# The head of the last product: GpSimd makes the sums of four weight chunks, and c's last pair but one takes its sums in another order

## The chip, the cores and the metric

One core of a Trainium2 chip runs the whole program. The metric is the device time of one execution in microseconds, the median of several. TensorE (PE) multiplies, VectorE (DVE), ScalarE (ACT) and GpSimd (POOL) do the elementwise work, and SyncE (SP) issues the transfers. Every engine works through its own list of instructions in order; an instruction whose operand isn't ready holds up everything behind it on its engine.

## The reference

```python
attn = softmax(causal(q @ k.T / 8)) @ v        # 2 x 12 heads, 448 x 64
x = attn, as 896 tokens x 768
h = x @ w_in;  g = h * cos(h)                  # 768 -> 2048
y = g @ w_out                                  # 2048 -> 768
a = y @ w_a;   b = y @ w_b                     # 768 -> 1536 each
out = (a * b) @ w_o2                           # c = a * b;  1536 -> 768
```

All of it is in float32. The last product (o2 in the kernel) is `c @ w_o2`.

## The kernel before

**Two halves.** A float32 operand is used as a pair: hi, the value rounded to the matmul's type, written by ScalarE, and lo, the rest, written by VectorE or GpSimd. One block product is three matmuls: hi by hi, hi by lo, lo by hi. So nothing is multiplied before the hi and lo of both sides are there.

**Weights.** They arrive as 88 chunks, numbered i in the order of use; the last product has 18 of them, from `o2_first` = 70 on, six for each of its three column pairs p. A chunk lies in HBM as 64-bit numbers. For each one: `w_scale` (two ScalarE instructions, the second into a PSUM tile named top, of which there is one), `w_bits` (two VectorE instructions, line 202), `w_sums` (below), `w_hi` (ScalarE, in two parts of 384 and 512 columns) and `w_lo` (GpSimd, the same two parts). When `w_lo(i)` is done, the load of chunk i+4 is issued into the same place. The calls are written out by hand among the matmuls: `halves_of(i)` makes `w_bits` up to i, the scale of the next one and then hi and lo of i; `bits_to(i)` makes only the scales and bits up to i.

**Seven products for eight.** The last product and most of `a` multiply 2x2 blocks with seven products. It needs sums of blocks on both sides. For a chunk, `w_sums` (lines 144 to 150) makes them in three instructions, each of which needs the one before: a difference of 128x128, two sums at once in 128x256, and a difference of 128x128. In the kernel before VectorE makes all three for a chunk of the last product. For c, each pair q = 0..5 of row blocks has four blocks (b11, b12, b21, b22) and the sums t1, t3, t2, t4.

**c.** a is made first and kept; each product b_q lands in four PSUM banks and is multiplied with a. For q from 3 on (`c_mult_psum`) b12 is multiplied in its PSUM bank, and `sum_psum` makes t3 in b12's bank, and t2 and then t4 in b22's bank. `half` makes hi and lo: from PSUM with VectorE, from SBUF with GpSimd. `steps_of` is the list of these steps ("+t2" the sum, "t2" its hi and lo), taken from `todo` by `items(n)`. t4 overwrites t2 in its bank, so it must wait until t2's halves are made.

**PSUM.** `bank(next(cycle), ...)` hands out seven banks in turn. The last product opens seven products at once. By that cycle its b11, t2 and t3 get the banks of b12, b21 and b22 of q = 4; its t1 and b21 those of b11 and b21 of q = 5; and its b22 and t4 those of b12 (which holds t3) and b22 (which holds t2, then t4) of q = 5. A product can't begin before VectorE has read its bank for the last time.

**The place.** Of the products a and b, b_4 and b_5 are the last. b_5 is multiplied in two batches, first b11 and b21, then b12 and b22 (lines 861 to 882). At the head of the last product (lines 898 to 911) c's last pair q = 5 is split, and TensorE multiplies all seven products for chunks 70 and 71 (42 matmuls), then chunks 72 and 73 (21 each), then 74 and 75 in turn. Places for new tiles of c come from the list `free`, first in, first out.

Of the kernel before, what the change touches and what calls it, by code (L numbers as in the profile page):

```python
# [14 lines left out]
ALU = mybir.AluOpType  # L15
# [15 lines left out]
def tile_causal_attention_cos_gate_bilinear(  # L31
# [16 lines left out]
    nc = tc.nc  # L48
# [5 lines left out]
    N_IN, N_Y, N_Q = w_in.shape[0], w_out.shape[0], w_a.shape[0]  # L54
# [17 lines left out]
    T_Y = N_Y // 2  # L72
    FIRST_PLAIN = 1
    AB = [("a", 0), ("b", 0), ("a", 1), ("b", 1), ("a", 2), ("a", 3), ("b", 2), ("a", 4), ("a", 5), ("b", 3), ("b", 4), ("b", 5)]
# [66 lines left out]
    def w_sums(i):  # L141


        if is_seven(*queue[i][:2]):
            t = f32(raw[i]).rearrange("p (s n) w -> p s w n", s=4)
            nc.vector.tensor_tensor(out=t[:, 0, 1], in0=t[:, 0, 0], in1=t[:, 1, 0], op=ALU.subtract)  # L146
            a22 = t[:, 2, 0].unsqueeze(1).to_broadcast([P, 2, P])
            nc.vector.tensor_tensor(out=t[:, 1:3, 1], in0=t[:, 0], in1=a22, op=ALU.add)  # L148
            engine = nc.gpsimd if i < o2_first else nc.vector
            engine.tensor_tensor(out=t[:, 3, 1], in0=t[:, 3, 0], in1=t[:, 2, 1], op=ALU.subtract)  # L150

    def w_parts(i):

# [51 lines left out]
    def w_halves(i):  # L205

        w_hi(i)
        w_lo(i, nc.gpsimd)
# [131 lines left out]
    with ExitStack() as actx:  # L340
# [11 lines left out]
        for o in (0, S):  # L352
            for e in range(2):
                half = mask[e * D : (e + 1) * D, o : o + D]
                nc.gpsimd.affine_select(
                    out=half,
# [232 lines left out]
    with tc.manual_schedule():  # L589
# [35 lines left out]
        def get(kind, q, name, part=""):  # L625
            return tiles[kind, q, name, part][0]
# [24 lines left out]
        def items(n):  # L651
            while n and todo:
                if next(todo[0], todo) is todo:
                    todo.popleft()
                else:
                    n -= 1
# [50 lines left out]
        def bits_to(i):  # L707
            while bits[0] <= i:
                scale_next()
                w_bits(bits[0])  # L710
                bits[0] += 1

        def halves_of(i):
            bits_to(i)
            scale_next()
            w_halves(i)
# [41 lines left out]
        def multiply_plain(kind, p, q, batches, use):  # L758
            for r in range(2):
                for b in batches:  # L760
                    name = name_of(r, b)
                    if q == 0:
                        banks[name] = bank(next(cycle), f"{kind}_{name}")[:, :S]
                    for k in range(2):
                        x_pair = pair_of("y", q, name_of(k, b))
                        terms(banks[name], chunks[kind, p, q][:2], BLOCK[r, k], x_pair, q == k == 0, q == T_Y - 1 and k == 1)
                    if q == T_Y - 1:
                        use(p, name, banks[name])
# [6 lines left out]
            nc.vector.tensor_tensor(out=t, in0=ps, in1=t, op=ALU.mult)  # L775

        in_psum = {}

        def c_mult_psum(p, name, ps):

            if name[2] == "2":
                in_psum[p, name] = ps
            if name == "b12":
                nc.vector.tensor_tensor(out=ps, in0=ps, in1=get("c", p, name), op=ALU.mult)
                drop("c", p, name)
            else:
                c_mult(p, name, ps)

        def sum_psum(q, name):
            t3, t2 = in_psum[q, "b12"], in_psum[q, "b22"]  # L790
            if name == "t1":
                ops = make("c", q, "t1"), t3, get("c", q, "b11")
            elif name == "t3":
                ops = t3, t3, get("c", q, "b22")
            elif name == "t2":
                ops = t2, get("c", q, "b11"), t3
            else:
                ops = t2, get("c", q, "b21"), t2
            nc.vector.tensor_tensor(out=ops[0], in0=ops[1], in1=ops[2], op=ALU.subtract)  # L799

        def half(q, name, dve):
            key = {"t3": "b12", "t2": "b22", "t4": "b22"}.get(name)
            src = in_psum[q, key] if (q, key) in in_psum else get("c", q, name)
            engine = nc.vector if name in dve or (q, key) in in_psum else nc.gpsimd
            split(src, (make("c", q, name, "hi"), make("c", q, name, "lo")), engine)
            if (q, key) not in in_psum:
                drop("c", q, name)

        def steps_of(q, steps, dve=()):
            for step in steps.split():  # L810
                if step[0] == "+":
                    sum_psum(q, step[1:])
                else:
                    half(q, step, dve)
                yield
# [9 lines left out]
        for turn, (kind, p) in enumerate(AB[:-1]):  # L825
            banks, kept = {}, {}
            for q in range(T_Y):
                halves_of(n + 3)
                bits_to(n + 4)
                items(PER_QUAD[turn])  # L830
                if n == o2_first - T_Y - 1:
                    bits_to(n + 5)
                if is_seven(kind, p):
                    for name in OPS:
                        multiply(kind, p, q, [name], "y", T_Y)
                        if q == T_Y - 1:
                            take(name, banks[name], lambda m: make("c", p, m), lambda m, t: None)
                else:
                    use = a_copy if kind == "a" else c_mult if p < OWN else c_mult_psum
                    multiply_plain(kind, p, q, ALL, use)  # L840
                del chunks[kind, p, q]
                n += 1
            if kind == "b" and p < OWN:
                split_c(p, () if p < 2 else ("b11", "b21", "b22"))
            elif kind == "b":
                todo.append(steps_of(p, "+t1 +t3 +t2 t2 +t4 t3 t4 b11 b21 b22 t1"))
                items(3)
            if (kind, p) == ("a", N_Q - 1):
                for t in range(T_Y):
                    for name in T_NAMES:  # L850
                        for part in ("hi", "lo"):
                            drop("y", t, name, part)
        assert n + T_Y == o2_first

        def drop_batch(b):
            for t in range(T_Y):
                for m in range(2):
                    for part in ("hi", "lo"):
                        drop("y", t, name_of(m, b), part)
# [1 line left out]
        banks = {}  # L861
        last = N_Q - 1
        for q in range(T_Y):
            items((2, 1, 0)[q])
            if q == 0:
                halves_of(o2_first)
            if q == 1:
                bits_to(o2_first + 2)
            multiply_plain("b", last, q, [0], c_mult_psum)
        drop_batch(0)  # L870
        for q in range(T_Y):
            if q == 1:
                scale_next()
            items((3, 2, 0)[q])
            if q == 1:
                bits_to(o2_first + 3)
            multiply_plain("b", last, q, [1], c_mult_psum)
            del chunks["b", last, q]
            if q < 2:
                w_halves(o2_first + 1 + q)  # L880
# [17 lines left out]
        for p in range(T_Y):  # L898
            banks, kept = {}, {}
            i = o2_first + p * N_Q  # L900
            if p == 0:
                todo.append(steps_of(last, "+t1 +t3 +t2 t2 +t4 t3 t4 b11 b21 b22 t1", ("b21",)))
                w_halves(i + 3)
                items(7)
                bits_to(i + 4)
                items(4)
                all_done()
                for name in OPS:
                    for q in range(2):
                        multiply("o2", p, q, [name], "c", N_Q)  # L910
                del chunks["o2", p, 0], chunks["o2", p, 1]
                halves_of(i + 4)
            for q in range(0 if p else 2, DOUBLE):
                halves_of(i + q + 3)
                if (p, q) not in ((0, 3), (1, 0), (1, 1)):
                    bits_to(i + q + 4)
                multiply("o2", p, q, OPS, "c", N_Q)
                del chunks["o2", p, q]
            for step, name in enumerate(OPS):
                for q in range(DOUBLE, N_Q):  # L920
                    multiply("o2", p, q, [name], "c", N_Q)
                take(name, banks[name], result, lambda m, t: store(p, m, t))
                if step == (5 if p == 0 else 0):
                    halves_of(i + DOUBLE + 3)
                if step == 6 and p:
                    bits_to(i + N_Q + 2)
            for q in range(DOUBLE, N_Q):
                del chunks["o2", p, q]
            halves_of(i + N_Q + 2)
            if p:  # L930
                bits_to(i + N_Q + 3)
# [56 lines left out]
```

## Time and profile before

| | us |
|---|---|
| median of 3 runs | 568.85 |
| lowest and highest | 567.16, 568.89 |
| the profiled execution | 566.28 |
| its span in the trace | 564.5 |
| TensorE busy | 552.3 |
| VectorE busy | 413.4 |
| ScalarE busy | 327.2 |
| GpSimd busy | 314.5 |

The span runs from the first to the last instruction of the trace, and the profiled execution's own time is 1.8 us longer. All times of instructions below are from the span's start. Busy time is summed over the whole span; where a wait lies is told by the view of waits and by the lists in order of time.

### The profile page before, as it was taken

What the parts mean: (1) busy time and instruction counts of PE and PEld (TensorE: products, weight loads), DVE (VectorE), ACT (ScalarE), POOL (GpSimd) and SP (SyncE); (2) the same over time, 40 slices, a digit from 0 to 9 for tenths busy, and PEclk for the clock granted to TensorE, in tenths of its full rate; (3) what the DMA queues carried; (4) which work ended last, traced back from release to release, by engine and by line L of the source; (5) the groups of instructions that cost most, each with busy time, mean ns of one, the idle gap of its engine ahead of it and who ended that gap; (6) DMA issues with size and microseconds to landing.
All of it is one profiled execution on the core that took longest, in us unless ns stands there. A gap on an engine that the chain in (4) does not pass through costs nothing.

```text
span 564.5 us, 9012 instructions
## 1 busy us (share of the span) xinstructions
PE 552.3 (98%) x3195; PEld 493.1 (87%) x3195; DVE 413.4 (73%) x752; ACT 327.2 (58%) x675; POOL 314.5 (56%) x307
## 2 busy tenths in 40 slices
PE   8999999999999999999999999999999999599997
PEld 5676689999999999999999999999999999599996
DVE  5899937777777775753742768898787878879994
ACT  6888937777777743322233865675544546545650
POOL 4557743666666652322231895998552656655651
PEclk9999999999999999999999999999999999799999
DMA  8845211333333234342441335244344321334431
GB/s 320 303 135 220 91 57 57 111 113 111 112 107 99 89 119 149 95 130 76 131 148 39 112 84 177 77 133 128 111 121 140 108 82 47 102 113 144 145 103 66
DMA packets 18045, 67.82 MB, mean 120 GB/s; under 512 B 2000, under 2 KB 3664, under 8 KB 18000
## 3 DMA queue, kind: packets, MB, share of 16 engines
q1 hardware_dynamic: 18000, 67.25, 36.6%
q8 instruction: 25, 0.41, 0.3%
q14 instruction: 20, 0.16, 0.1%
HBM read 64.49 MB, written 2.75 MB: 119 GB/s over the span
## 4 chain that ended last, share of the span: by engine, by line
PE 84%; DVE 7%; ACT 4%; issue 2%; POOL 2%; POOLq 0%; DVEq 0%; ACTq 0%
PE h L232 21%; PE y L232 21%; PE b_b L746 9%; PE a_b L746 7%; PE o_t L746 7%; PE a_t L746 6%; PE o_b L746 6%; PE xa L507 2%; PE pt L480 2%; PE s L405 2%; POOL p L467 1%; DVE p L428 1%; ACT p L452 1%; DVE b_b L799 1%; DVE c_b L775 1%
## 5 line engine op out<-in xcount | busy, mean ns | idle before, releaser
L175 POOL TENSOR_TENSOR w_lo<-w_raw,w_hi 128x512 fp32r<-128x512 f32 (+2 forms) x121 | 168.6, 1402 | 164.2 <-ACT w_hi L168 124.4
L168 ACT ACTIVATE w_hi<-w_raw 128x384 fp32r<-128x384 f32 (+2 forms) x118 | 80.0, 688 | 137.9 <-DVE w_raw L137 38.2
L114 ACT ACTIVATE w_raw<-w_raw 128x512 f32<-128x512 f32 (+1 forms) x88 | 65.2, 741 | 0.6 <-DMA w_raw<-in_w_b 0.6
L130 DVE SCALAR_TENSOR_TENSOR w_raw<-w_raw 128x768 int32<-128x768 int32 (+1 forms) x34 | 52.9, 1556 | 16.4 <-ACT w_raw L114 15.5
L467 POOL TENSOR_SCALAR p<-p,sums 128x448 f32<-128x448 f32 (+6 forms) x84 | 40.7, 505 | 26.9 <-DVE mn L428 25.5
L202 DVE SCALAR_TENSOR_TENSOR top<-w_raw,top 128x512 int32<-128x512 int32 x54 | 37.2, 688 | 18.8 <-ACT top L119 18.1
L119 ACT ACTIVATE top<-w_raw 128x512 int32<-128x512 uint32 x54 | 34.0, 630 | 26.1 <-DVE w_raw L202 25.5
L452 ACT ACTIVATE p<-p,mn 128x448 f32<-128x448 f32 (+6 forms) x84 | 41.8, 501 | 7.8 <-DVE mn L428 7.8
L202 DVE SCALAR_TENSOR_TENSOR w_raw<-w_raw,top 128x512 int32<-128x512 int32 x54 | 37.2, 690 | 5.4
L272 DVE SCALAR_TENSOR_TENSOR r<-r,h 128x448 f32<-128x448 int32 x32 | 19.7, 616 | 25.8 <-ACT r L271 25.7
L428 DVE CUSTOM_DVE_ANT_0 p<-s,mask 128x448 f32<-128x448 f32 (+6 forms) x84 | 32.0, 415 | 3.8 <-PE s L405 3.6
L137 DVE SCALAR_TENSOR_TENSOR w_raw<-w_raw 128x768 int32<-128x768 int32 (+1 forms) x34 | 31.6, 931 | 0.4
L405 PE MATMUL s<-qk_raw 64*64 64x448 f32 (+6 forms) x336 | 26.8, 390 | 0.7 <-DVE mn L428 0.5
L148 DVE TENSOR_TENSOR w_raw<-w_raw 128x256 f32<-128x256 f32 x33 | 25.5, 774 | 1.1
L271 ACT ACTIVATE r<-h 128x448 int32<-128x448 f32 x32 | 17.2, 540 | 15.9 <-PE h L232 8.2
L405 PEld LDWEIGHTS s<-qk_raw 64*64 64x64 f32 x336 | 15.2, 132 | 11.2 <-issue 3.7
L480 PE MATMUL pt<-ident,p 128*128 128x128 f32 x168 | 23.9, 280 | 1.0 <-POOL p L467 0.6
L507 PEld LDWEIGHTS xa<-pp,v 128*64 128x64 f32 x336 | 16.1, 137 | 9.4 <-issue 7.1
L507 PE MATMUL xa<-pp,v 128*64 128x64 f32 (+3 forms) x336 | 23.8, 293 | 0.0
L146 DVE TENSOR_TENSOR w_raw<-w_raw 128x128 f32<-128x128 f32 x33 | 22.5, 681 | 1.1
L480 PEld LDWEIGHTS pt<-ident,p 128*128 128x128 f32 x168 | 18.2, 140 | 3.7 <-POOL p L467 2.0
L124 DVE TENSOR_SCALAR w_raw<-w_raw 128x768 int32<-128x768 int32 (+1 forms) x34 | 21.2, 623 | 0.0
(374 smaller groups left out, 1717.3 us busy)
## 6 DMA issues: line engine op xcount, KB each, us to landing
w_raw<-in_w_in SPq DMA_DIRECT2D x16, 768.0 KB, 4.4
w_raw<-in_w_out SPq DMA_DIRECT2D x12, 768.0 KB, 4.3
w_raw<-in_w_a SPq DMA_DIRECT2D x18, 512.0 KB, 3.6
w_raw<-in_w_b SPq DMA_DIRECT2D x18, 512.0 KB, 3.6
w_raw<-in_w_o SPq DMA_DIRECT2D x18, 512.0 KB, 3.8
v<-in_v SPq DMA_DIRECT2D x12, 448.0 KB, 5.8
qk_raw<-in_qk SPq DMA_DIRECT2D x11, 448.0 KB, 5.7
w_raw<-in_w_out SPq DMA_DIRECT2D x6, 512.0 KB, 3.8
```

The source lines that it names most:

```text
L114: nc.scalar.activation(high, high, ACTF.Copy, scale=2.0**-112)
L130: nc.vector.scalar_tensor_tensor(out=low, in0=high, scalar=3, in1=low, op0=ALU.logical_shift_left, op1=ALU.bitwise_or)
L168: nc.scalar.activation(pair[0][:, a:z], src, ACTF.Copy)
L175: engine.tensor_tensor(out=lo[:, a:z], in0=src, in1=f32(hi)[:, a:z], op=ALU.subtract)
L202: nc.vector.scalar_tensor_tensor(out=out_, in0=high, scalar=by, in1=top, op0=op, op1=ALU.bitwise_or)
L232: nc.tensor.matmul(ps, w[:, c * P : (c + 1) * P], acts[t + c][part], start=t == 0 and i == 0, stop=t + k == n and i == len(terms) - 1,)
L405: nc.tensor.matmul(T["s", i + c][q, o : o + WIDTH[j]], t[h, Q_COL[j] : Q_COL[j] + D], t[h, FIRST[j] : FIRST[j] + WIDTH[j]], start=True, st ...
L452: nc.scalar.activation(t, t, ACTF.Exp, bias=T["mn", n][:, c], scale=-1.0, accum_out=row_sum(n, j))
L467: nc.gpsimd.tensor_scalar(out=t, in0=t, scalar1=row_sum(n, j), scalar2=1.0, op0=ALU.mult, op1=ALU.mult)
L480: nc.tensor.transpose(dst, p_bufs[n % N_P][:, o : o + P], ident)
L507: nc.tensor.matmul(ps[e * D : (e + 1) * D, o * D : w * D], t[:, k, e], p[:, :, :, q].rearrange("p s l q -> p (s l) q") if k < 3 else p[:, ...
L746: nc.tensor.matmul(ps, w_part, x_part, start=start and i == 0, stop=stop and i == 2)
```

## The change

`w_sums`: for the first four chunks of the last product (70 to 73) GpSimd makes all three sums; from chunk 74 on VectorE does, as before. For the chunks of `a` VectorE makes the first two and GpSimd the third, as before.

c's pair q = 4: t4 goes into b21's PSUM bank and no longer overwrites t2, so all four sums are made at once; the order of the steps behind them is another. In the products b_3 and b_4 the steps of c are issued ahead of `bits_to`. `items` and `bits_to` of b_5's two batches are moved, `free` is turned so that the places that the first batch gives up are used first, and at the head of the last product the seven first steps of q = 5 come ahead of `w_halves` of chunk 73.

```diff
             a22 = t[:, 2, 0].unsqueeze(1).to_broadcast([P, 2, P])
-            nc.vector.tensor_tensor(out=t[:, 0, 1], in0=t[:, 0, 0], in1=t[:, 1, 0], op=ALU.subtract)
-            nc.vector.tensor_tensor(out=t[:, 1:3, 1], in0=t[:, 0], in1=a22, op=ALU.add)
-            engine = nc.gpsimd if i < o2_first else nc.vector
-            engine.tensor_tensor(out=t[:, 3, 1], in0=t[:, 3, 0], in1=t[:, 2, 1], op=ALU.subtract)
+            most = nc.gpsimd if o2_first <= i < o2_first + 4 else nc.vector
+            last = nc.vector if i >= o2_first + 4 else nc.gpsimd
+            most.tensor_tensor(out=t[:, 0, 1], in0=t[:, 0, 0], in1=t[:, 1, 0], op=ALU.subtract)
+            most.tensor_tensor(out=t[:, 1:3, 1], in0=t[:, 0], in1=a22, op=ALU.add)
+            last.tensor_tensor(out=t[:, 3, 1], in0=t[:, 3, 0], in1=t[:, 2, 1], op=ALU.subtract)
...
+        T4_BANK = {q: "b21" if q == N_Q - 2 else "b22" for q in range(N_Q)}
...
-                ops = t2, get("c", q, "b21"), t2
+                ops = in_psum[q, T4_BANK[q]], get("c", q, "b21"), t2
...
                 halves_of(n + 3)
+                if turn == len(AB) - 2:
+                    items(PER_QUAD[turn])
                 bits_to(n + 4)
-                items(PER_QUAD[turn])
-                if n == o2_first - T_Y - 1:
+                if turn < len(AB) - 2:
+                    items(PER_QUAD[turn])
+                elif q == T_Y - 1:
                     bits_to(n + 5)
...
-                todo.append(steps_of(p, "+t1 +t3 +t2 t2 +t4 t3 t4 b11 b21 b22 t1"))
-                items(3)
+                order = "+t1 +t3 +t2 t2 +t4 t3 t4 b11 b21 b22 t1"
+                todo.append(steps_of(p, order if p < N_Q - 2 else "+t1 +t3 +t2 +t4 b11 b21 t3 t2 t4 b22 t1"))
+                items(3 if p < N_Q - 2 else 4)
...
         for q in range(T_Y):
-            items((2, 1, 0)[q])
             if q == 0:
                 halves_of(o2_first)
+                items(2)
             if q == 1:
                 bits_to(o2_first + 2)
             multiply_plain("b", last, q, [0], c_mult_psum)
+        k = len(free)
         drop_batch(0)
+        free.rotate(-k)
         for q in range(T_Y):
-            if q == 1:
+            if q == 0:
                 scale_next()
             items((3, 2, 0)[q])
-            if q == 1:
+            if q == 2:
                 bits_to(o2_first + 3)
...
+                items(7)
                 w_halves(i + 3)
-                items(7)
```

**VectorE, between c's pair q = 4 and the last sums of q = 5.** c_b, c_t are tiles of c, b_b the PSUM banks of b, L146 to L150 the sums of a chunk, L202 its bits. Before:

```order
L212 TENSOR_TENSOR c_t4lo<-b_b_4545,c_t4hi 128x448
L202 SCALAR_TENSOR_TENSOR top<-w_raw,top 128x512
L202 SCALAR_TENSOR_TENSOR w_raw<-w_raw,top 128x512
L146 TENSOR_TENSOR w_raw<-w_raw 128x128
L148 TENSOR_TENSOR w_raw<-w_raw 128x256
L150 TENSOR_TENSOR w_raw<-w_raw 128x128
L784 TENSOR_TENSOR b_b_4731<-b_b_4731,c_b_4327 128x448
L775 TENSOR_TENSOR c_b_4338<-b_b_4738,c_b_4338 128x448
L799 TENSOR_TENSOR c_t_4808<-b_b_4731,c_b_4322 128x448
L799 TENSOR_TENSOR b_b_4731<-b_b_4731,c_b_4338 128x448
L799 TENSOR_TENSOR b_b_4738<-c_b_4322,b_b_4731 128x448
L212 TENSOR_TENSOR c_t2lo<-b_b_4738,c_t2hi 128x448
```

The same place now, on the same engine:

```order
L213 TENSOR_TENSOR c_t4lo<-b_b_4538,c_t4hi 128x448
L203 SCALAR_TENSOR_TENSOR top<-w_raw,top 128x512
L203 SCALAR_TENSOR_TENSOR w_raw<-w_raw,top 128x512
L785 TENSOR_TENSOR b_b_4734<-b_b_4734,c_b_4327 128x448
L776 TENSOR_TENSOR c_b_4338<-b_b_4741,c_b_4338 128x448
L800 TENSOR_TENSOR c_t_4801<-b_b_4734,c_b_4322 128x448
L800 TENSOR_TENSOR b_b_4734<-b_b_4734,c_b_4338 128x448
L800 TENSOR_TENSOR b_b_4741<-c_b_4322,b_b_4734 128x448
L213 TENSOR_TENSOR c_t2lo<-b_b_4741,c_t2hi 128x448
```

The three sums of chunk 73 are gone from between its bits and the products of c's pair q = 5; what follows stands in the same order.

**GpSimd, from the lo of chunk 69 to the lo of chunk 71.** w_lo is a chunk's lo, c_b11lo and c_b21lo those of c's pair q = 4. Before:

```order
L175 TENSOR_TENSOR w_lo<-w_raw,w_hi 128x512
L175 TENSOR_TENSOR w_lo<-w_raw,w_hi 128x384
L175 TENSOR_TENSOR w_lo<-w_raw,w_hi 128x512
L212 TENSOR_TENSOR c_b11lo<-c_b_4210,c_b11hi 128x448
L212 TENSOR_TENSOR c_b21lo<-c_b_4220,c_b21hi 128x448
L175 TENSOR_TENSOR w_lo<-w_raw,w_hi 128x384
```

And now:

```order
L151 TENSOR_TENSOR w_raw<-w_raw 128x128
L176 TENSOR_TENSOR w_lo<-w_raw,w_hi 128x384
L176 TENSOR_TENSOR w_lo<-w_raw,w_hi 128x512
L213 TENSOR_TENSOR c_b11lo<-c_b_4210,c_b11hi 128x448
L213 TENSOR_TENSOR c_b21lo<-c_b_4220,c_b21hi 128x448
L149 TENSOR_TENSOR w_raw<-w_raw 128x128
L150 TENSOR_TENSOR w_raw<-w_raw 128x256
L151 TENSOR_TENSOR w_raw<-w_raw 128x128
L176 TENSOR_TENSOR w_lo<-w_raw,w_hi 128x384
```

The sums of chunks 70 and 71 (their last row stands first here) come ahead of the lo of chunk 70, those of chunk 72 ahead of the lo of chunk 71, and, further on, those of chunk 73 between the lo of chunks 72 and 73.

## Rows read from the trace of the kernel before

**Rows 1.** The page: busy time and share of each engine.

```profile
PE 552.3 (98%) x3195; PEld 493.1 (87%) x3195; DVE 413.4 (73%) x752; ACT 327.2 (58%) x675; POOL 314.5 (56%) x307
```

**Rows 2.** TensorE's waits from 400 us on: us in total, times, longest.

```profile
PE o_b L746 <- DVE c_t3lo L212: 5.9, 1, 5.9
```

**Rows 3.** TensorE's list: start, duration, line, tiles, idle time before.

```profile
475.75 0.36 PE L746 MATMUL b_b<-y_b22hi,w_lo 128*128 128x448 f32 x1
...
481.83 0.36 PE L746 MATMUL o_b<-c_b21hi,w_lo 128*128 128x448 f32 x1
488.08 0.74 PE L746 MATMUL o_b<-c_b22hi,w_hi 128*128 128x448 f32 x1 [5.89 <-DVE c_t3lo L212]
...
492.43 0.37 PE L746 MATMUL o_b<-c_b11hi,w_hi 128*128 128x448 f32 x1
```

**Rows 4.** Stretches: PE, PEld, DVE, ACT, POOL busy (count); granted clock; DMA share; GB/s.

```profile
482.00:484.00 2.00, 0.19 (x1) 0.00 (x0) 2.00 (x4) 0.67 (x1) 2.00 (x3) 1.00 0.17 31
...
486.00:488.00 2.00, 0.00 (x0) 0.00 (x0) 1.66 (x3) 1.08 (x3) 0.00 (x0) 0.50 0.68 223
...
490.00:492.00 2.00, 2.00 (x7) 1.74 (x7) 1.93 (x3) 2.00 (x5) 2.00 (x2) 0.50 0.00 0
492.00:494.00 2.00, 2.00 (x11) 1.87 (x10) 1.97 (x3) 1.04 (x3) 2.00 (x3) 0.99 0.00 0
```

**Rows 5.** VectorE's list ahead of and in TensorE's wait.

```profile
459.21 0.41 DVE L146 TENSOR_TENSOR w_raw<-w_raw 128x128 f32<-128x128 f32 x1
...
462.16 0.68 DVE L202 SCALAR_TENSOR_TENSOR top<-w_raw,top 128x512 int32<-128x512 int32 x1
...
463.68 0.30 DVE L146 TENSOR_TENSOR w_raw<-w_raw 128x128 f32<-128x128 f32 x1
...
464.67 0.62 DVE L775 TENSOR_TENSOR c_b<-b_b,c_b 128x448 f32<-128x448 f32 x1
...
473.80 0.66 DVE L146 TENSOR_TENSOR w_raw<-w_raw 128x128 f32<-128x128 f32 x1
...
476.73 1.14 DVE L775 TENSOR_TENSOR c_b<-b_b,c_b 128x448 f32<-128x448 f32 x2
...
479.83 0.54 DVE L146 TENSOR_TENSOR w_raw<-w_raw 128x128 f32<-128x128 f32 x1
...
482.78 0.62 DVE L784 TENSOR_TENSOR b_b<-b_b,c_b 128x448 f32<-128x448 f32 x1
483.32 0.61 DVE L775 TENSOR_TENSOR c_b<-b_b,c_b 128x448 f32<-128x448 f32 x1
...
487.41 0.62 DVE L212 TENSOR_TENSOR c_t3lo<-b_b,c_t3hi 128x448 fp32r<-128x448 f32 x1
488.17 0.62 DVE L212 TENSOR_TENSOR c_t4lo<-b_b,c_t4hi 128x448 fp32r<-128x448 f32 x1
```

**Rows 6.** GpSimd's instructions of line 150: duration in ns, least/median/most, first and last start.

```profile
L150 POOL TENSOR_TENSOR w_raw<-w_raw x15: 515/523/835, 323.9 to 414.3; 128x128 f32<-128x128 f32 x15
```

**Rows 7.** GpSimd's list.

```profile
460.60 1.48 POOL L175 TENSOR_TENSOR w_lo<-w_raw,w_hi 128x512 fp32r<-128x512 f32 x1
470.87 2.32 POOL L175 TENSOR_TENSOR w_lo<-w_raw,w_hi 128x384 fp32r<-128x384 f32 x2 [8.79 <-ACT w_hi L168]
...
475.43 2.55 POOL L175 TENSOR_TENSOR w_lo<-w_raw,w_hi 128x384 fp32r<-128x384 f32 x2
477.94 1.17 POOL L212 TENSOR_TENSOR c_b22lo<-c_b,c_b22hi 128x448 fp32r<-128x448 f32 x1
...
497.55 2.31 POOL L175 TENSOR_TENSOR w_lo<-w_raw,w_hi 128x384 fp32r<-128x384 f32 x2 [1.43 <-ACT w_hi L168]
```

**Rows 8.** ScalarE's list behind the products of q = 5.

```profile
487.60 0.54 ACT L211 ACTIVATE c_t4hi<-b_b 128x448 fp32r<-128x448 f32 x1 [0.92 <-DVE b_b L799]
488.04 0.67 ACT L114 ACTIVATE w_raw<-w_raw 128x512 f32<-128x512 f32 x1
```

**Rows 9.** The page: loads of the last product's chunks, us from issue to landing.

```profile
w_raw<-in_w_o SPq DMA_DIRECT2D x18, 512.0 KB, 3.8
```

More of the change, by code (lines that the diff above doesn't have):

```diff
@@ L777, in tile_causal_attention_cos_gate_bilinear @@
         in_psum = {}
+        T4_BANK = {q: "b21" if q == N_Q - 2 else "b22" for q in range(N_Q)}
         def c_mult_psum(p, name, ps):
-            if name[2] == "2":
-                in_psum[p, name] = ps
+            in_psum[p, name] = ps
             if name == "b12":
@@ L797, in sum_psum @@
             else:
-                ops = t2, get("c", q, "b21"), t2
+                ops = in_psum[q, T4_BANK[q]], get("c", q, "b21"), t2
             nc.vector.tensor_tensor(out=ops[0], in0=ops[1], in1=ops[2], op=ALU.subtract)
         def half(q, name, dve):
-            key = {"t3": "b12", "t2": "b22", "t4": "b22"}.get(name)
+            key = {"t3": "b12", "t2": "b22", "t4": T4_BANK[q]}.get(name)
             src = in_psum[q, key] if (q, key) in in_psum else get("c", q, name)
```

## The prediction

> **What bounds the kernel now.** First the page: TensorE is busy for 552.3 us of a span of 564.5 [rows 1], so nearly all that can be won is its idle time and what it multiplies at the lower clock. Then TensorE's waits: from 400 us on there is a single one, 5.9 us, for VectorE's lo of t3 [rows 2]. Then TensorE's own list around it [rows 3]: the last matmul of b starts at 475.75, 30 matmuls of the last product follow at an even pace, (481.83 - 475.75) / 30 = 0.203 us each, and the product b22, due at 481.83 + 0.20 = 482.03, starts at 488.08. It wants the PSUM bank that holds t3 of q = 5, and VectorE's last read of that bank ends at 487.41 + 0.62 = 488.03 [rows 5]. The clock comes next [rows 4]: granted 1.00 (2.4 GHz) at 482 to 484, 0.50 (1.2 GHz) at 486 to 488, after TensorE has stood still, still 0.50 at 490 to 492 with TensorE busy throughout, and 0.99 from 492 on. So the 12 matmuls from 488.08 to 492.43 took 4.35 us [rows 3], where 12 at 0.203 are 2.43.
>
> The price of the place is then: idle 488.08 - 482.03 = 6.05 us, clock 4.35 - 2.43 = 1.92 us, together 7.97 us. It is also the most that an edit here can win.
>
> Why was VectorE late? Its last product of q = 5 starts at 483.32 [rows 5], though TensorE had filled that bank by 475.75 + 0.36 = 476.11 [rows 3]: 7.2 us late. Ahead of it in VectorE's list stand the sums of chunks 70 to 73. From 483.32 to the end of t3's lo at 488.03 are 4.71 us, to that of t4's lo (488.17 + 0.62 = 488.79) 5.47 us.
>
> **The change part by part.**
>
> *Sums off VectorE.* The four groups of three took, from their first start to the next instruction's: 459.21 to 462.16, 2.95 us; 463.68 to 464.67, 0.99; 473.80 to 476.73, 2.93; 479.83 to 482.78, 2.95 [rows 5]. Together 9.82 us leave VectorE's list ahead of the product of b12 at 482.78, which could so start at 472.96. TensorE fills b12's bank only six matmuls before the last, at 476.11 - 1.22 = 474.89, and b22's at 476.11. So VectorE will be waiting for TensorE there and no longer the other way round, and the price is paid once more from 476.15: eight instructions in the same order as before, t3's lo done at 476.15 + 4.71 = 480.86, t4's lo at 476.15 + 5.47 = 481.62. TensorE wants those banks at 482.03 and, six matmuls later, at 483.25. Both waits go, with 1.17 and 1.63 us to spare. To win it all, 6.05 of the 9.82 us must arrive at the product of b12; 3.77 us may be lost on the way with nothing felt.
>
> *Other steps that VectorE waits for.* q = 4: t4 in a bank of its own takes away a wait of VectorE for ScalarE between two sums; its halves now take the places that the first batch gives up, free 36 matmuls before the end of b, at 475.95 - 7.31 = 468.64. Three hi on ScalarE, three lo of 0.62, and the bits of chunk 73 (two of 0.68) fit ahead of 474.89 with some 2 us to spare. I cost these edits at nothing; if that cover is gone they take from the 3.77 us first. The turned list `free` changes which older reader a tile waits for; those readers end near 478 (GpSimd's t1 of q = 4), ahead of their use at 480.4. Nothing again, and at most some tenths, below or above.
>
> *Sums onto GpSimd.* Of the three instructions its trace shows the last, 128x128: 0.52 us as a rule, 0.84 at most [rows 6]. The 128x256 one isn't shown there; it lies between one of 128x128 at its fastest, 0.52, and two at their slowest, 1.67. The lo of a chunk, 896 columns, takes 2.32 us [rows 7], 0.33 per 128 columns, so I take 0.52 + 0.33 = 0.85. A chunk's sums, X, are then 1.9 us, between 3 x 0.52 = 1.56 and 0.84 + 1.67 + 0.84 = 3.35. GpSimd had the room: it sat idle for 8.79 us until 470.87 [rows 7].
>
> Does it come in time? The lo of chunk 69 ended at 460.60 + 1.48 = 462.08; I put it 1 us later, since the bits of chunk 68 now stand behind q = 3's halves. Then sums of 70 and 71 until 466.9, lo of 70 (2.32) 469.2, two lo of c (1.17 each) 471.5, sums of 72 473.4, lo of 71 (2.55) 476.0. TensorE wants its second part at the 12th matmul of the last product, 475.95 + 11 x 0.203 = 478.2: 2.2 us to spare. On: two lo of c 478.3, lo of 72 480.9 (wanted at 484.9), sums of 73 482.8, lo of 73 485.3 (wanted at 489.1). The loads of chunks 73 to 76 start when the lo of 69 to 72 are done; 3.8 us each [rows 9] leave several us, and SyncE's list is as before.
>
> *What is late next.* ScalarE's scale of chunk 74 followed t4's hi at once, 488.04 [rows 8]. t4's hi moves by 476.15 - 483.32 = -7.17 us to 480.4, but between them now stands the hi of chunk 73, whose second part waits for GpSimd's sums (482.8); it ends near 483.4. All that follows on ScalarE, VectorE and GpSimd stands in the old order, so it runs 488.04 - 483.4 = 4.6 us earlier, TensorE 7.97. The lo of chunk 75, done at 497.55 + 2.31 = 499.86 before [rows 7], comes at 495.2. TensorE wants its second part 12 + 42 + 11 = 65 matmuls behind 482.03: 495.2. No spare, and no loss; each 0.1 us on X is 0.4 us here, as four chunks' sums stand ahead. I take the loss at 0, with 0 to 4 x (3.35 - 1.9) = 5.8 us as bounds; below 0 it can't go, since TensorE has no other idle time there to win.
>
> One rule speaks against the change. First the rows: the sums took 0.99 us on VectorE when GpSimd was idle and 2.93 to 2.95 when it was at work [rows 5]. The Trainium skill says in "SBUF — State Buffer" (SBUF: two separate sides) that GpSimd and a VectorE instruction with two inputs from SBUF exclude each other on a shared port, and in "Perfetto Trace Analysis" (Optimizing Scalar/DVE Operations) that moving work between the two might therefore not help. The trace bears out the first for the sums. What stays on VectorE in this stretch reads one input from PSUM, though, and such an instruction took 0.62 us at 482.78 with GpSimd busy for all 2 us, and 0.62 at 487.41 with GpSimd idle [rows 4, 5]; so by the rows nothing comes back, and by the rule taken for all VectorE work the sum would be near 0. That is a rival below.
>
> The Trainium skill's "GPSIMD Engine Reference" (3.1 Elementwise) has GpSimd about twice as slow as VectorE at two-input work and advises VectorE. By that the estimate would be 2 x 0.99, about 2 us a chunk, near the X taken here; but it is 2.9 us that leave VectorE.
>
> **Sum.** 566.28 - 6.05 - 1.92 = 558.3 us for the profiled execution. That one lies 2.57 us below the median of the runs shown and 0.9 below the lowest; taken from the median, 568.85 - 7.97 = 560.9 us. This I predict.
>
> **Rivals.**
>
> 1. *GpSimd comes late, but not by much.* X lies above 1.9, and chunk 75, then chunk 71, are waited for. For it: no spare for chunk 75, a 128x256 sum that the trace doesn't show. Against it: GpSimd's lo varied only between 2.32 and 2.55 [rows 7]. Loss 1 to 5.8 us: 562 to 566.7. Chance 0.15.
>
> 2. *Moved, not won.* VectorE's other work stretches beside a busier GpSimd, or ScalarE's new order holds it up, by about as much as is freed; the wait for t3 stays. For it: 0.99 against 2.95 [rows 5]. Against it: the two durations of 0.62. 568 to 569. Chance 0.06.
>
> 3. *Slower: GpSimd becomes the bound of the head.* The sums need each other and stand ahead of the lo in one list; beyond a certain X, TensorE waits for the lo of chunks 71 and 75 for longer than it did for t3. Each us on X costs 4; it decides from 4 x (X - 1.9) = 7.97, X = 3.9, and is measurably slower from X = 4.3. At X = 5: 12.4 - 7.97 = 4.4 us more, 573.3. For it: four times three dependent instructions are added. Against it: the rows end at 3.35. Chance 0.04.
>
> **Numbers.** Forecast, the whole price won: 0.75, with 559 to 562 as its own range (the runs before spread by 1.7 us). The whole range, 558.5 to 564.5, takes in the likelier half of rival 1 and leaves the rest out. A difference of 0.3%, 1.7 us, is about what a measurement of this kernel can tell from none: faster 0.75 + 0.15 = 0.90, within it 0.06, slower 0.04.
>
> **What will show it.** Right: no TensorE wait for t3's lo, the granted clock 1.00 throughout 476 to 500, the product b22 at 482.0 and the first matmul of chunk 72 at 484.5; VectorE idle ahead of the product of b12, which starts at 474.9 on TensorE's release; the sums on GpSimd at 0.5, 0.85 and 0.5 us. Wrong: 128x256 on GpSimd above 1.7 us; a TensorE wait for GpSimd's w_lo near 478 or 495; VectorE's list still full ahead of 476; matmuls at the lower clock anywhere in the head.

## The result, and the profile after

| | before | changed |
|---|---|---|
| median, us | 568.21 (4 runs, 567.16 to 568.89) | 559.34 (4 runs, 558.93 to 559.74) |
| the profiled execution, and its span | 566.28, 564.5 | 558.97, 556.5 |
| last matmul of b starts | 475.75 | 475.76 |
| last matmul of the kernel starts | 560.47 | 552.50 |

The ratio is 0.9845, 95% interval [0.9824, 0.9866]: faster, by 8.9 us in the medians and 8.0 us in the spans. The two last rows of the table say where: up to the end of b the two executions are level, and from there to the last matmul the changed kernel takes 76.74 us instead of 84.72, 7.98 less. I call this stretch the tail; it leaves out the beginning of a run, which shifts by up to 0.8 us from one execution to another, so single profiles are compared by it below.

The page's first line after [rows 1]: TensorE is busy for 2.6 us less, since matmuls at the lower clock are gone, and the rest of the 8 us was idle time.

```profile
PE 549.7 (99%) x3195; PEld 491.6 (88%) x3195; DVE 403.6 (73%) x740; ACT 327.7 (59%) x675; POOL 321.0 (58%) x319
```

TensorE's waits, now over the whole span (us in total, times, longest). All three lie far ahead of the last product; the wait for t3's lo [rows 2] is gone and none has taken its place.

```profile
PE s L406 <- DVE mn L429: 1.2, 1, 1.2
PE warm L528 <- POOL zeros L344: 1.0, 1, 1.0
PE pt L481 <- POOL p L468: 0.6, 2, 0.4
```

The stretches, with the columns of [rows 4]. TensorE is busy throughout and the granted clock stays at 1.00, also where it was 0.50.

```profile
482.00:484.00 2.00, 2.00 (x12) 1.85 (x11) 0.01 (x1) 1.79 (x4) 2.00 (x3) 1.00 0.43 170
486.00:488.00 2.00, 2.00 (x12) 1.85 (x11) 1.97 (x2) 1.42 (x3) 2.00 (x2) 1.00 0.60 213
...
490.00:492.00 2.00, 2.00 (x12) 1.85 (x11) 1.86 (x5) 0.95 (x2) 0.86 (x1) 1.00 0.07 16
492.00:494.00 2.00, 2.00 (x12) 1.85 (x10) 1.86 (x4) 1.85 (x4) 1.77 (x2) 1.00 0.73 244
```

TensorE's list [rows 3]: the end of b, the product b22, the first matmul of chunk 72, and the one that first reads the second part of chunk 75's lo.

```profile
475.76 0.36 PE L747 MATMUL b_b<-y_b22hi,w_lo 128*128 128x448 f32 x1
...
482.04 0.37 PE L747 MATMUL o_b<-c_b22hi,w_hi 128*128 128x448 f32 x1
...
484.47 0.36 PE L747 MATMUL o_b<-c_b11hi,w_hi 128*128 128x448 f32 x1
...
495.21 0.37 PE L747 MATMUL o_t<-c_t2hi,w_lo 128*128 128x448 f32 x1
```

VectorE's list [rows 5]. The product of b12, which came 482.78 - 474.89 = 7.9 us after its bank was full, now waits 2.46 us for TensorE, and that of b22 0.58 us, where it had come 7.2 us late; t3's lo is done at 480.27 + 0.61 = 480.88 and t4's at 481.65, each over a microsecond ahead of its matmul.

```profile
474.94 0.63 DVE L785 TENSOR_TENSOR b_b<-b_b,c_b 128x448 f32<-128x448 f32 x1 [2.46 <-PE b_b L747]
476.16 0.62 DVE L776 TENSOR_TENSOR c_b<-b_b,c_b 128x448 f32<-128x448 f32 x1 [0.58 <-PE b_b L747]
...
480.27 0.61 DVE L213 TENSOR_TENSOR c_t3lo<-b_b,c_t3hi 128x448 fp32r<-128x448 f32 x1
481.03 0.62 DVE L213 TENSOR_TENSOR c_t4lo<-b_b,c_t4hi 128x448 fp32r<-128x448 f32 x1
```

GpSimd's list [rows 7]: the sums of chunk 72 from 471.34 to 473.37, 2.03 us, then the lo of 71; the lo of 73; the lo of 75.

```profile
471.34 0.53 POOL L149 TENSOR_TENSOR w_raw<-w_raw 128x128 f32<-128x128 f32 x1
471.95 0.86 POOL L150 TENSOR_TENSOR w_raw<-w_raw 128x256 f32<-128x256 f32 x1
472.89 0.52 POOL L151 TENSOR_TENSOR w_raw<-w_raw 128x128 f32<-128x128 f32 x1
473.37 2.31 POOL L176 TENSOR_TENSOR w_lo<-w_raw,w_hi 128x384 fp32r<-128x384 f32 x2
...
482.13 2.33 POOL L176 TENSOR_TENSOR w_lo<-w_raw,w_hi 128x384 fp32r<-128x384 f32 x2
...
492.23 2.33 POOL L176 TENSOR_TENSOR w_lo<-w_raw,w_hi 128x384 fp32r<-128x384 f32 x2 [1.38 <-ACT w_hi L169]
```

The middle sum by engine, from the view of line 150: duration in ns, least/median/most. This is the price that the trace before didn't show [rows 6]; VectorE's row has all its chunks, with GpSimd idle and at work.

```profile
L150 DVE TENSOR_TENSOR w_raw<-w_raw x29: 425/427/1433, 322.4 to 542.5; 128x256 f32<-128x256 f32 x29
L150 POOL TENSOR_TENSOR w_raw<-w_raw x4: 854/858/863, 463.4 to 480.7; 128x256 f32<-128x256 f32 x4
```

And ScalarE at the head [rows 8]: the hi of chunk 73, which waits for GpSimd's sums, and behind it the scale of chunk 74, 5.2 us earlier than before.

```profile
482.21 0.68 ACT L169 ACTIVATE w_hi<-w_raw 128x512 fp32r<-128x512 f32 x1 [0.77 <-POOL w_raw L151]
482.80 0.65 ACT L114 ACTIVATE w_raw<-w_raw 128x512 f32<-128x512 f32 x1
```

### The profile page after: what moved, and what is told of

It reads as the page before. It is cut to its first block, busy times and chain, and to the rows that moved or that the text cites. A ratio compares the mean times of both kernels' runs of the same rounds, so it can differ in the third digit from the quotient of the medians.

```text
span 556.5 us, 9006 instructions
## 1 busy us (share of the span) xinstructions
PE 549.7 (99%) x3195; PEld 491.6 (88%) x3195; DVE 403.6 (73%) x740; ACT 327.7 (59%) x675; POOL 321.0 (58%) x319
## 4 chain that ended last, share of the span: by engine, by line
PE 93%; DVE 2%; ACT 2%; POOL 1%; issue 1%; POOLq 0%; DVEq 0%
PE h L233 21%; PE y L233 21%; PE b_b L747 16%; PE o_t L747 8%; PE a_b L747 8%; PE a_t L747 7%; PE o_b L747 6%; PE xa L508 2%; PE pt L481 2%; PE s L406 2%; ACT p L453 2%; POOL p L468 1%; DVE p L429 1%; PE warm L528 1%; DVE pp L494 0%
## 5 line engine op out<-in xcount | busy, mean ns | idle before, releaser
L150 DVE TENSOR_TENSOR w_raw<-w_raw 128x256 f32<-128x256 f32 x29 | 21.5, 740 | 1.0
L149 DVE TENSOR_TENSOR w_raw<-w_raw 128x128 f32<-128x128 f32 x29 | 20.6, 710 | 1.0
```

## The experiments

The theory: VectorE's list was too long by the sums, and taking them off pays the whole price of the place, as long as GpSimd has its lo of the chunks in time. The rivals: the order of the steps does it and not the sums; fewer chunks would do; GpSimd's time is closer to the limit than the result shows. The kernels e1 to e4 ran on one chip (before: 567.42 us there, 8 runs), e5 to e8 on another (before: 567.64 us, 9 runs), and each ratio is to the kernel before on the same chip. The last four columns are of the profiled execution. "b22" is the time from the last matmul of b to the first of the product b22; 6.28 us, 31 matmuls at the even pace, is no wait. "Wait" is TensorE's from 400 us on.

| kernel | median, us | ratio to before [95%] | wait, us | lowest clock behind it | b22, us | tail, us |
|---|---|---|---|---|---|---|
| before | 568.21 | | 5.9 | 0.50 | 12.33 | 84.72 |
| changed | 559.34 | 0.9845 [0.9824, 0.9866] | 0 | 1.00 | 6.28 | 76.74 |
| e1 sums only | 562.10 | 0.9917 [0.9900, 0.9933] | 2.0 | 1.00 | 8.46 | 79.06 |
| e2 order only | 565.18 | 0.9960 [0.9946, 0.9973] | 3.0 | 0.50 | 9.47 | 82.78 |
| e3 two chunks | 562.83 | 0.9926 [0.9911, 0.9941] | 2.1 | 1.00 | 8.37 | 79.92 |
| e4 sum made twice | 564.20 | 0.9950 [0.9932, 0.9969] | 2.5 | 1.00 | 6.74 | 81.06 |
| e5 sums and one move | 560.95 | 0.9882 [0.9867, 0.9897] | 1.0 | 1.00 | 6.27 | 78.11 |
| e6 without that move | 564.36 | 0.9947 [0.9931, 0.9963] | 2.9 | 0.50 | 9.35 | 81.51 |
| e7 sum made four times | 571.14 | 1.0060 [1.0045, 1.0075] | 7.1 | 0.50 | 14.92 | 88.38 |
| e8 three chunks | 559.20 | 0.9849 [0.9834, 0.9864] | 0 | 1.00 | 6.28 | 76.78 |

**e1: the sums alone.** The kernel before, with only `w_sums` of the change.

```diff
-            nc.vector.tensor_tensor(out=t[:, 0, 1], ...)
-            nc.vector.tensor_tensor(out=t[:, 1:3, 1], ...)
-            engine = nc.gpsimd if i < o2_first else nc.vector
...
+            most = nc.gpsimd if o2_first <= i < o2_first + 4 else nc.vector
+            last = nc.vector if i >= o2_first + 4 else nc.gpsimd
...
```

> The kernel before with nothing but the sums of chunks 70 to 73 on GpSimd; c's steps, banks, places and the order of the calls are as before. Theory A (the 9.8 us of sums were all that made VectorE late): the wait for t3's lo is gone and the whole 8 us are won, a profile near 556.5 us of span. Theory B (the order is needed as well): ScalarE's hi of chunk 73 still stands ahead of t2's hi of q = 5 and now waits for GpSimd's sums of chunk 73, which end near 481; t2's hi then starts near 482, t3's lo ends near 483.7 to 484.5, and TensorE still waits 1.7 to 2.5 us at 482.03 for it, too short a stand for the clock to fall as before; span 558 to 559.

It won 5.66 of the 7.98 us. TensorE still waits for t3's lo, but for 2.0 us instead of 5.9, and the clock isn't lost. In ScalarE's list the rest is seen: the second part of chunk 73's hi stands ahead of the hi of t2, and waits 4.75 us for GpSimd's sums of that chunk. The first row is TensorE's.

```profile
485.02 0.47 PE L747 MATMUL o_b<-c_b22hi,w_hi 128*128 128x448 f32 x1 [2.01 <-DVE c_t3lo L213]
482.08 0.67 ACT L169 ACTIVATE w_hi<-w_raw 128x512 fp32r<-128x512 f32 x1 [4.75 <-POOL w_raw L151]
482.66 0.52 ACT L212 ACTIVATE c_t2hi<-b_b 128x448 fp32r<-128x448 f32 x1
```

So the move of the sums makes a new wait, on ScalarE, and another edit of the change must have taken it away.

**e2: the order alone.** The changed kernel with the sums of 70 to 73 on VectorE.

```diff
-            most = nc.gpsimd if o2_first <= i < o2_first + 4 else nc.vector
-            last = nc.vector if i >= o2_first + 4 else nc.gpsimd
+            most = nc.gpsimd if False else nc.vector
+            last = nc.vector if i >= o2_first else nc.gpsimd
```

> The changed kernel with the sums of chunks 70 to 73 back on VectorE; all other edits are kept. Theory A (it is VectorE's load): 9.8 us return to its list; of them the new order hides some, since VectorE waited 5 us in all for ScalarE there before; t3's lo ends between 483.5 and 486 and TensorE waits 1.5 to 4 us; the clock falls only if it stands for about 3 us; span 558 to 562. Rival (the order alone makes the gain): no wait, span 556.5. Rival (moved, not won): wait as before, span 564.5.

It won 1.94 us of the tail. VectorE's product of b12 starts only at 480.69 there, behind 3.16 us of sums of chunk 73, TensorE waits 3.0 us and the clock falls. The third row is TensorE's, the last has the granted clock (third number from the right) behind the wait:

```profile
477.53 0.90 DVE L149 TENSOR_TENSOR w_raw<-w_raw 128x128 f32<-128x128 f32 x1
...
480.69 0.62 DVE L785 TENSOR_TENSOR b_b<-b_b,c_b 128x448 f32<-128x448 f32 x1
485.99 0.47 PE L747 MATMUL o_b<-c_b22hi,w_hi 128*128 128x448 f32 x1 [3.03 <-DVE c_t3lo L213]
...
488.00:490.00 2.00, 2.00 (x7) 1.79 (x6) 1.76 (x3) 2.00 (x6) 2.00 (x3) 0.50 0.14 20
```

The first rival is out: the order is a part, the smaller one. The span, 563.8 us, lies above the 558 to 562 that I had put down. From 490 us on TensorE issues its matmuls at a slower pace than in the changed kernel (see e3), which costs 1.2 us of this tail; without it the order alone would have won some 3.1 us (an estimate, 1.94 + 1.2).

**e3: two chunks.** Only 70 and 71 on GpSimd, the rest as changed.

```diff
-            most = nc.gpsimd if o2_first <= i < o2_first + 4 else nc.vector
-            last = nc.vector if i >= o2_first + 4 else nc.gpsimd
+            most = nc.gpsimd if o2_first <= i < o2_first + 2 else nc.vector
+            last = nc.vector if i >= o2_first + 2 else nc.gpsimd
```

> The changed kernel with only the sums of chunks 70 and 71 on GpSimd, those of 72 and 73 on VectorE. My sum says 6.05 of the 9.8 us have to leave VectorE and 3.77 may stay; here 3.9 us leave by the old trace (2.95 + 0.99), 5.9 stay. By the old list alone TensorE would wait about 2 us. If the new order has freed VectorE of its waits for ScalarE as well, the sums of 73 end near 476 to 477, b22's product starts 0 to 1 us late, and t3's lo still comes at 481 to 482: no wait or under 0.3 us, span 556.5 to 557.

It lost 3.18 us against the change, most of it by a wait of 1.94 us for t3's lo. VectorE's list shows why: the sums of chunk 73 take 2.98 us beside GpSimd, and the product of b12 follows them at 479.65, far behind TensorE, which had filled its bank before the end of b. The last row is TensorE's.

```profile
476.67 0.56 DVE L149 TENSOR_TENSOR w_raw<-w_raw 128x128 f32<-128x128 f32 x1
477.27 1.14 DVE L150 TENSOR_TENSOR w_raw<-w_raw 128x256 f32<-128x256 f32 x1
478.44 1.28 DVE L151 TENSOR_TENSOR w_raw<-w_raw 128x128 f32<-128x128 f32 x1
479.65 0.62 DVE L785 TENSOR_TENSOR b_b<-b_b,c_b 128x448 f32<-128x448 f32 x1
...
484.94 0.47 PE L747 MATMUL o_b<-c_b22hi,w_hi 128*128 128x448 f32 x1 [1.94 <-DVE c_t3lo L213]
```

By b22's start 2.09 us are lost. Some 0.5 follow at the restart and in a 0.2 us wait for a chunk's lo at 524.15, and 0.6 in the pace behind that: from here

```profile
524.66 0.37 PE L747 MATMUL o_t<-c_t3lo,w_hi 128*128 128x448 f32 x1
...
556.49 0.37 PE L747 MATMUL o_t<-c_t4hi,w_lo 128*128 128x448 f32 x1
```

154 matmuls take 31.83 us, 0.207 us each, where the changed kernel takes 552.50 - 521.29 = 31.21 us for the same ones, 0.203 each, with a granted clock of 1.00 in both. e4 and e7 have this slower pace in the same place, e2 from 490 us on; before, e1, e5, e6 and e8 don't have it there. What sets it these runs don't show.

**e8: three chunks.** As e3, with `o2_first + 3`: only the sums of 73 go back to VectorE.

> The changed kernel with the sums of chunks 70 to 72 on GpSimd and those of 73 on VectorE. VectorE stood idle for 2.46 us ahead of b12's product in the changed kernel; three sums beside a busy GpSimd take 2.9 to 3.0. Theory: b12's product starts about 0.5 us late, b22's on TensorE's release as before, t3's lo still at 480.9; no wait, the time from the last matmul of b to the end within 0.2 us of the changed kernel's 76.7, and chunk 75's lo earlier by up to 2 us. Rival (VectorE's spare is less than that): TensorE waits 0.5 us or more for t3's lo.

Equal to the change, within 0.04 us of tail. The product of b12 still waits for TensorE, though only for 0.21 us:

```profile
475.69 0.63 DVE L785 TENSOR_TENSOR b_b<-b_b,c_b 128x448 f32<-128x448 f32 x1 [0.21 <-PE b_b L747]
```

e3 and e8 stand on the two sides of the limit: with the new order, two chunks off VectorE's list are too few, and the fourth is spare.

**e6: the change without one move.** At the head of the last product `w_halves(i + 3)` comes ahead of `items(7)` again, as before the change.

```diff
-                items(7)
                 w_halves(i + 3)
+                items(7)
```

> The changed kernel with one edit undone: at the head the hi and lo of chunk 73 stand ahead of the seven steps of q = 5 again. Theory: ScalarE's hi of chunk 73 waits for GpSimd's sums until about 482.2, t2's hi starts at 482.9 in place of 478.6, t3's lo ends near 484.3 in place of 480.9, TensorE waits 2.0 to 2.5 us, the clock stays at 1.00; 2.2 to 2.8 us more than the changed kernel, about 562. Rival (the move brings nothing): as the changed kernel.

It lost 4.77 us. This is the edit that e1 lacked. TensorE's wait, and ScalarE's list, in which the hi of t2 stands behind the hi of chunk 73:

```profile
485.81 0.47 PE L747 MATMUL o_b<-c_b22hi,w_hi 128*128 128x448 f32 x1 [2.91 <-DVE c_t3lo L213]
482.87 0.67 ACT L169 ACTIVATE w_hi<-w_raw 128x512 fp32r<-128x512 f32 x1 [5.65 <-POOL w_raw L151]
483.44 0.53 ACT L212 ACTIVATE c_t2hi<-b_b 128x448 fp32r<-128x448 f32 x1
```

VectorE, ready at 479.2, then waits 4.85 us for that hi:

```profile
484.07 0.62 DVE L213 TENSOR_TENSOR c_t2lo<-b_b,c_t2hi 128x448 fp32r<-128x448 f32 x1 [4.85 <-ACT c_t2hi L212]
```

I had expected a shorter wait and the clock to stay. It fell as well: of the 4.77 us, 3.07 are in b22's start (9.35 - 6.28) and 1.70 behind it.

**e5: the sums and that one move, nothing else of the change.** e1 with `items(7)` ahead of `w_halves(i + 3)`.

```diff
-                w_halves(i + 3)
                 items(7)
+                w_halves(i + 3)
```

> The kernel before with two edits alone: the sums of chunks 70 to 73 on GpSimd, and the seven steps of q = 5 ahead of the hi of chunk 73. Theory (these two are the whole gain, the bank of t4, the turned places and the other moves cost and bring nothing): no wait for t3's lo, the time from the last matmul of b to the last of the kernel within 0.3 us of the changed kernel's 76.7 us; median about 559 to 560. Rival (t4's own bank and the moves matter): TensorE waits 0.5 us or more for t3's lo, 77.3 us or more.

b22 starts in time, so the two edits together pay the whole price of the place. But the tail is 1.37 us longer than with the change, where I had expected next to no difference: TensorE now waits for chunk 75's lo (0.6 us, here) and once more at 522.56 (0.4 us).

```profile
496.35 0.47 PE L747 MATMUL o_t<-c_t2hi,w_lo 128*128 128x448 f32 x1 [0.57 <-POOL w_lo L176]
```

In GpSimd's list of e5 are idle times that the changed kernel doesn't have, 1.57 us for ScalarE's hi of chunk 70 and 0.66 for VectorE's bits of chunk 72:

```profile
467.88 2.31 POOL L176 TENSOR_TENSOR w_lo<-w_raw,w_hi 128x384 fp32r<-128x384 f32 x2 [1.57 <-ACT w_hi L169]
470.85 0.52 POOL L149 TENSOR_TENSOR w_raw<-w_raw 128x128 f32<-128x128 f32 x1 [0.66 <-DVE w_raw L203]
```

They are 2.2 us in the head of the list, and what stands behind is later: the lo of chunk 73 ends 10.0 us behind the last matmul of b, with the change 8.7. So the remaining edits together (t4's bank, `free`, the moves around b_3 to b_5) are worth these 1.37 us; that they win them by feeding GpSimd earlier is read from the two lists, and which of them does it I did not try one by one.

**e4 and e7: heavier sums on GpSimd.** The changed kernel, with the middle sum written twice, and four times, on GpSimd; the values are the same.

```diff
-            most.tensor_tensor(out=t[:, 1:3, 1], in0=t[:, 0], in1=a22, op=ALU.add)
+            for _ in range(2 if most is nc.gpsimd else 1):   # e7: 4
+                most.tensor_tensor(out=t[:, 1:3, 1], in0=t[:, 0], in1=a22, op=ALU.add)
```

> The changed kernel with the 128x256 sum on GpSimd made twice for each of the four chunks (the second writes the same): X grows from 1.9 to 2.85 us a chunk. Theory (GpSimd has almost no spare at chunk 75, and each us on X costs 4 behind that): the lo of chunk 75 moves from 494.6 to about 497 to 498.3, wanted at 495.2; TensorE waits 1.5 to 3 us for GpSimd's or ScalarE's work on chunk 75, span 558 to 559.5. Rival (GpSimd has room): no wait, 556.5.

> The changed kernel with the 128x256 sum on GpSimd made four times for each of the four chunks (the same values): X grows from 1.95 to about 4.8 us a chunk. By my price of 4 us for each us on X, less 0.65 us of spare at chunk 75, TensorE waits 4 x 2.85 - 0.65 = 10.7 us more than in the changed kernel, in several places (chunks 71, 73, 75); by the slope of the run with the sum made twice (4.3 us for 0.94) up to 14. Span 567 to 571, slower than the kernel before: the point from which GpSimd turns the gain into a loss lies below 4.8. Rival (the waits overlap and the loss levels off): under 8 us, span below 564.5.

The sums of chunk 72, with 2.03 us in the changed kernel, took 476.68 - 473.75 = 2.93 us in e4 and 481.75 - 477.06 = 4.69 us in e7; the tail grew by 4.32 and 11.64 us. In e4 0.3 us are lost at 477.78, at the matmul that first reads chunk 71's lo; the longest wait is at chunk 75, for its hi, which ScalarE makes late:

```profile
496.43 0.47 PE L748 MATMUL o_b<-c_b11hi,w_hi 128*128 128x448 f32 x1 [1.71 <-ACT w_hi L170]
```

In e7 the main wait comes much sooner, for the lo of chunk 71, six matmuls behind the end of b:

```profile
482.82 0.74 PE L748 MATMUL o_b<-c_b11hi,w_lo 128*128 128x448 f32 x1 [5.62 <-POOL w_lo L177]
```

The waits of e4, 2.5 us, were within what I had put down, and its span of 561.3 us above it; in e7 the waits came to 7.1 us and not 10.7, but 2.8 us more went at the lower clock behind the first of them, and the span, 568.2 us, was within.

So GpSimd can become the bound, and then the same change is slower than the kernel before: e7 by 0.6%, interval above 1. A straight line between e4 and e7 (an estimate) reaches the 7.98 us that the change won at 2.93 + (7.98 - 4.32) x 1.76 / 7.32 = 3.8 us a chunk.

## Why the prediction was right

**The price of the place.** 6.05 us idle and 1.92 us of clock, 7.97 together; the tail is 7.98 shorter. The median, forecast at 560.9 us, came out at 559.34, near the lower end of 559 to 562: it fell by 8.87 us, and the 0.9 us beyond the tail lie within the spread of the runs (1.7 us before). The product b22 was due at 482.03 and starts at 482.04; chunk 72 was due at 484.5 and starts at 484.47.

**VectorE.** That the sums leave, that VectorE then waits for TensorE, and that t4's lo is done eight instructions behind the end of b, was right to within 0.04 us: product of b12 at 474.94 (474.9), t3's lo done at 480.88 (480.86), t4's at 481.65 (481.62). That 6.05 of the 9.82 us must arrive and 3.77 may be lost agrees with the runs, which only bracket it: e3, which takes away 3.9 us of the old list, fails; e8, which takes 6.9, doesn't. My own expectation for e3 (next to nothing lost) went against that bound, and the bound held: beside GpSimd's work the sums of chunks 72 and 73 cost VectorE 3.47 and 2.98 us in e3.

**Sums onto GpSimd.** 0.85 us was taken for the 128x256 sum, and 0.854 to 0.863 were measured; X is 2.03 with the gaps between dependent instructions, where I had 1.9. The lo of 70, 71, 72 and 73 were forecast for 469.2, 476.0, 480.9 and 485.3 and ended at 469.17, 475.68, 480.17 and 484.46: the longer X was more than made up, because the lo of chunks 71 to 73 took 2.30 to 2.33 us each, where I had taken about 2.5. The Trainium skill's "GPSIMD Engine Reference" (3.1 Elementwise) has GpSimd about twice as slow at such work. The trace agrees, 858 against 427 ns in the medians of the two rows of line 150, and 427 is VectorE undisturbed (its least is 425, its longest 1433); the point is that it was not undisturbed here.

**Chunk 75.** Forecast without spare; its lo ended at 494.56 and TensorE took it at 495.21, 0.65 us to spare. The lists behind the scale of chunk 74 had moved by 5.2 us, where I had taken 4.6. The step's slope, 4 us for each us on X, holds at this chunk. Less the spare it gives 4 x 0.90 - 0.65 = 2.95 us in e4 and 4 x 2.66 - 0.65 = 9.99 us in e7. The 100th matmul behind the end of b, just past those that waited for chunk 75, starts 20.26 us behind it in the changed kernel, 23.47 in e4 and 30.76 in e7, so 3.21 and 10.50 us later. The rest of the two tails, 1.1 us in each, is a later wait (0.5 us) and the slower pace (0.6). So rival 1's place and rival 3's mechanism are real. That rival 3's point of decision, 3.9, stands beside 3.8 of the runs is in part luck: the 0.65 us of spare that it left out and the 1.1 us behind chunk 75 that it didn't know pull against each other. What kept both away is that X was 2.0.

**Moved, not won.** The Trainium skill's rule on the shared port ("SBUF — State Buffer", SBUF: two separate sides), which the prediction weighed, is borne out for the sums and not for VectorE's work that reads PSUM. With GpSimd busy all the time VectorE's instructions with one input in PSUM took 0.61 to 0.63 us, as before. The sums that stayed on VectorE still pay: those of chunk 74 took 0.40, 1.27 and 1.12 us, but nobody waits for them.

**What was incomplete.** The reorderings, costed at nothing. With all of them in, nothing was lost, so the sum came out, but not because I had seen what they pay; they are no ornaments. Without the move of `items(7)` the change wins 3.21 of its 7.98 us (e6), and without the others 6.61 (e5). I had seen what the move does to ScalarE's scale of chunk 74, and not that without it ScalarE's hi of chunk 73 would hold t2's hi back, which in e6 came 4.2 us after its sum was done (479.22 to 483.44). My expectations for e5 and e6 were off for the same reason.

## What to carry to other kernels

When an engine's list ends in a wait of TensorE, count how many microseconds must leave that list and how many only may; then price the sums where they stand, with the neighbour at work, since 1.0 us on VectorE was 3 there and 2.0 on GpSimd. When a step goes to another engine, look at once at every third engine that reads its result: an instruction that waits there holds up all that stands behind it, and here that decided over more than half of the gain. Then raise the moved step's cost on purpose once: it shows how much room is left: here 0.9 us more a chunk took over half of the gain, and by the estimate 1.8 us would take all of it.

## What the runs showed of the hardware

The clock stayed at 2.4 GHz (granted 1.00) after TensorE had stood still for 2.0 us (e1) and 1.9 us (e3), and fell to 1.2 GHz (0.50) after 2.9 (e6), 3.0 (e2), 5.6 (e7) and 5.9 us (before). These are the profiled executions. The expectations for e1 and e2 reckon with a length of stand from which on the clock falls; that isn't shown. The profiled executions would fit one, but the others aren't all alike: the mean granted clock of a whole execution was 1.00 in all four of e1, but 0.996 in two of e3's four, and 1.00 in one of e2's five. In e6 it fell only when TensorE was already at work again; the stretches behind its wait, which ended before 486:

```profile
486.00:488.00 2.00, 2.00 (x8) 1.76 (x8) 1.52 (x3) 2.00 (x5) 0.50 (x1) 0.67 0.81 250
488.00:490.00 2.00, 2.00 (x7) 1.78 (x6) 1.93 (x3) 2.00 (x5) 2.00 (x3) 0.50 0.03 12
```

So a wait can have two prices, without and with the clock: 2.0 us cost 2.3 of tail in e1 (79.06 - 76.74), 2.9 us cost 4.8 in e6. The other thing I had not expected is how one-sided the contention of VectorE and GpSimd is. Before, VectorE's sums of chunk 72 took 2.93 us, from 473.80 to 476.73, where those of chunk 71 had taken 0.99 beside an idle GpSimd [rows 5, 7]. In that stretch GpSimd was at two lo of c and began the lo of chunk 71, 2.55 us [rows 7]:

```profile
473.14 1.17 POOL L212 TENSOR_TENSOR c_b11lo<-c_b,c_b11hi 128x448 fp32r<-128x448 f32 x1
474.26 1.21 POOL L212 TENSOR_TENSOR c_b21lo<-c_b,c_b21hi 128x448 fp32r<-128x448 f32 x1
```

In the changed kernel, with the sums gone from VectorE, the same three took 1.15, 1.16 and 2.31 us. GpSimd had lost 0.31 us beside the sums, and VectorE 1.94.
